# A recurrence with a feed-forward network on one core: another issue order for the first third of the pieces

## The chip, the cores and the metric

The kernel runs on one core of a Trainium2 chip. The metric is the device time of one execution in microseconds (us); lower is better. The engines are named as in the profile: PE is TensorE's matmul, PEld its weight load, DVE is VectorE, ACT ScalarE, POOL GpSimd and SP SyncE, which only issues DMAs here. Each engine works off its own queue strictly in order; an instruction at the head that waits for another engine holds everything behind it.

## What is computed

Two blocks follow each other. The first is a recurrence over 768 steps on a 40 × 40 state for each of 4 × 8 heads:

```python
for t in range(S):
    kt, vt, rt = (k[:, :, t], v[:, :, t], r[:, :, t])
    wt, at, bt = (w[:, :, t], a[:, :, t], b[:, :, t])
    y[:, :, t] = np.einsum('bhd,bhde->bhe', rt, state)
    Sa = np.einsum('bhde,bhe->bhd', state, at)
    state_decay = state * wt[:, :, None, :] - np.einsum('bhd,bhe->bhde', Sa, bt)
    state = state_decay + np.einsum('bhd,bhe->bhde', vt, kt)
```

The second takes the 3072 tokens of 8 × 40 = 320 values through an RMS norm and a SwiGLU network of 1536 hidden units:

```python
rms = np.sqrt(np.mean(x * x, axis=-1, keepdims=True) + 1e-06)
xn = x / rms * rms_g
g = xn @ w_gate
silu = g * (1.0 / (1.0 + np.exp(-g)))
val = xn @ w_val
return (silu * val @ w_out).astype(np.float32)
```

The inputs of the recurrence are float32; the three weight matrices arrive as 64-bit floats and are narrowed to float32 on the chip.

## The kernel before

**Stages.** The 768 steps are cut into 24 chunks of 32. For each chunk c there are three stages. `front(c)` (L652) loads w, a, k and b, transposes them on TensorE, builds products over spans of 2, 4, 8 and 16 steps (K, A and Ab tiles, T for the decays), makes Gram matrices in PSUM ("gramk") and picks their masked parts into LT (`where`, the COPY_PREDICATED of the profile). It then stores LT to DRAM (tile sB) and loads it back in another layout as M. `inverse(c)` (L760), or for the first four chunks `early_inverse(c)` (L778), solves the triangular system of a chunk: a chain of short multiply and subtract pairs on VectorE, then a store to sY, a load back, and for the early chunks two groups of small matmuls ("inv"). `main(c)` (L810) applies the state, solves for the chunk's updates, updates the state and computes the output tokens, which it normalizes and transposes into xg. After every second chunk `feed(g)` (L939) takes 256 tokens through the network: for each of the 12 slices of hidden units it loads a slice of narrowed weights from sW and runs the matmuls "h64", "h" and "out".

**Narrowing.** `narrow(f, h)` (L973) makes one half of such a weight slice: two to four loads of raw 64-bit words on SP into a wf tile, three activations on ScalarE (the first reads the top 16 bits, `ex<-wf,ctop`), one tensor_scalar and two scalar_tensor_tensor on VectorE, and a store to sW. It runs once for each half slice and is spread over the first part of the program.

**Constants.** At the start GpSimd makes two index rows with `iota` (L537), from which VectorE makes the masks msk and near; GpSimd also fills the pads and fixed parts of tiles (`blank`, L478, the MEMSET rows of L479; `pcopy`, L475, the COPY rows of L476).

**Order.** None of these functions issues anything by itself. Each operation, or each group of matmuls with one purpose, becomes a piece in a `Plan` (L244), which notes what the piece reads and writes (`add`, L280). After all stages have been entered, `issue` (L322) emits the pieces in the order of the string `ORDER` (L33). A number n stands for the n-th piece after the first one that is not yet out, so 0 is the next in the order of entry; "-" issues one warm-up matmul (L1015), which multiplies the identity into a spare part of a PSUM tile. `PAIRS` (L228) has a digit for each use of PSUM: which of the three pairs of banks (ps0 to ps2) it gets. As each engine takes its instructions in program order, the string fixes the order of every engine's queue, and the order of DMAs on SP, ACT and POOL. The DMAs of the first chunks are issued from SP and ACT, later ones from POOL.

The diff touches the two strings alone; they are consumed here:

```python
        for word in order.split():
            if word == "-":
                self.order.append(None)
                self.warm()
                continue
            i = first + int(word)
```

Of the kernel before, what the change touches and what calls it, by code (L numbers as in the profile page):

```python
# [33 lines left out]
85 83 84 76 58 78 86 74 73 59 60 75 5 89 61 88 77 4 43 6 201 7 87 334 90 44 8 214 213 53 62 9 - - - - - - - - 93 18 10  # L34
567 335 557 11 12 13 79 14 15 94 566 80 210 16 95 558 108 17 200 - - - 97 96 19 20 100 21 2 22 101 23 98 25 568 202 24
26 107 112 57 - - - - - 102 106 111 124 27 209 122 392 103 109 52 119 113 104 54 578 569 577 155 199 125 110 105 204
120 - - - - - - 114 203 118 117 121 559 211 598 589 562 46 131 129 132 45 560 212 597 563 588 561 123 115 136 586 384
133 134 - - - - - 126 130 116 47 564 3 145 216 394 383 135 336 128 137 48 144 143 141 91 587 219 142 51 570 127 1005
565 146 138 337 55 573 579 281 393 220 582 608 571 390 234 239 607 572 583 580 380 574 251 222 38 221 609 575 581 42 -
- - - - - - - 223 82 226 339 64 379 227 338 39 81 139 224 263 149 576 238 153 56 249 247 590 206 584 228 382 237 591  # L40
593 272 40 233 232 381 154 0 593 32 139 390 204 228 591 388 234 249 247 - - 324 235 35 31 27 244 229 146 147 259 281
245 258 149 34 325 594 36 33 270 155 243 62 605 584 598 230 - 239 40 214 599 601 242 628 64 49 91 627 602 30 626 1135
600 28 48 257 603 29 241 68 150 255 65 0 1347 194 0 194 84 173 0 - - - 182 540 200 0 184 1 186 542 540 0 506 0 457 469
849 199 455 242 111 97 110 112 96 51 61 439 460 458 122 50 243 0 0 255 242 0 709 104 470 242 120 246 259 708 57 247
458 456 0 257 718 256 470 242 0 716 265 487 486 0 268 0 0 265 101 473 0 262 277 0 273 0 236 0 260 0 269 0 242 461 - -
- - - - - 237 0 240 0 278 242 252 0 242 252 0 90 0 0 98 99 246 0 0 230 440 0 230 94 93 457 440 231 - - - - - - - - -
240 441 244 0 44 0 468 440 255 0 450 468 269 469 0 257 214 439 238 213 203 0 257 203 93 449 92 0 0 234 - - - - - - - -
245 437 0 250 262 0 464 246 247 436 260 245 446 258 259 469 244 - - 255 471 465 468 470 466 0 269 215 255 478 466 93
94 264 95 96 266 97 0 97 470 1 2 98 99 0 0 96 467 97 469 98 468 251 265 99 470 100 471 101 441 102 103 258 104 105 260
106 - - - - - - - - - - - 0 106 107 471 108 0 108 502 503 472 0 108 109 110 111 0 0 0 0 0 - - 13 0 16 562 572 146 571  # L50
561 147 14 142 143 374 15 13 355 - - - 25 386 358 0 358 386 388 16 25 387 389 390 70 79 17 391 28 191 147 355 356 80
148 149 359 0 68 28 2 29 149 0 149 34 150 29 151 187 24 25 31 152 33 153 188 391 393 32 154 35 390 392 358 0 0 152 40
187 153 27 154 155 156 33 157 158 159 160 161 34 162 36 163 164 37 165 41 391 38 42 392 39 394 561 166 395 393 552 0
42 559 549 548 395 209 0 549 560 42 165 210 43 44 211 427 428 395 - - - 565 166 45 167 557 168 0 565 566 168 739 0 522
693 534 526 124 - - 0 526 124 139 0 535 681 682 579 0 535 545 547 140 536 138 141 0 547 545 555 543 578 0 558 520 567
- - - - - - 518 378 0 696 378 380 381 695 518 120 685 526 - - - - - - 522 686 379 527 382 136 530 383 554 529 121 - -
141 540 523 565 539 537 142 538 524 - - - - 145 525 148 534 149 152 154 551 535 147 555 - - 157 146 550 536 150 155
# [3 lines left out]
478 595 568 - - 35 830 594 567 820 38 36 - 476 37 571 366 570 0 605 356 433 434 435 436 120 437 0 317 318 319 320 441  # L61
321 322 323 355 456 324 458 459 442 4 357 325 457 326 327 443 328 0 443 328 329 330 331 357 0 35 0 330 2 37 450 359 3
36 358 331 332 357 333 356 0 462 330 461 464 448 331 332 468 364 447 463 31 467 476 458 333 365 334 335 0 425 439 441
302 426 436 0 6 439 2 0 435 332 2 436 443 444 0 448 332 442 334 443 333 340 449 0 32 297 329 342 330 - 3 338 33 341
334 0 332 331 0 332 293 441 0 438 0 436 293 333 336 295 337 309 438 338 1 375 342 310 365 374 515 27 292 0 362 26 28
44 339 29 34 292 27 32 338 0 646 29 34 336 32 0 439 64 315 647 646 339 440 441 63 340 0 287 413 312 313 623 12 414 314
415 315 416 608 624 32 417 480 418 625 419 420 421 316 626 638 33 0 312 417 625 418 - - - - 476 313 601 602 600 610
812 419 420 421 822 258 422 423 0 313 810 423 625 637 2 0 819 2 0 254 473 420 421 645 310 422 0 - - - - - 310 422 3
313 33 0 28 626 307 419 639 627 420 637 308 0 637 20 635 420 647 21 421 23 422 613 648 819 38 22 809 423 39 659 24 611
3 612 36 818 424 651 808 621 425 25 660 426 - 616 249 427 0 427 3 25 58 57 428 28 47 0 428 429 28 430 3 431 0 26 25  # L70
614 484 31 27 617 627 0 458 216 400 590 600 401 0 12 582 32 401 583 25 0 397 579 21 - - - - - - - - - 588 29 28 30 591
22 453 428 398 605 23 0 591 23 429 602 24 609 0 24 397 588 602 1 604 398 429 430 2 399 427 0 584 - - - - - - - - - - -
- - - 4 397 0 25 397 4 0 393 394 21 23 27 28 395 598 24 424 607 0 21 38 35 395 37 396 24 2 424 47 397 398 399 400 25
# [4 lines left out]
663 729 634 977 562 563 717 713 986 978 665 564 565 566 975 567 568 714 569 985 570 571 967 722 572 723 - 0 400 403  # L78
726 402 572 401 573 0 726 738 736 573 739 574 664 575 737 576 577 3 723 578 751 579 760 580 747 581 582 633 583 584 0
584 585 3 634 586 636 587 635 734 588 633 0 746 588 - - - - - 403 757 589 722 590 3 404 591 592 593 594 595 596 408  # L80
# [967 lines left out]
```

## Time and profile before

| | |
|---|---|
| three runs | 1069.33, 1063.34, 1067.66 us |
| median of the three | 1067.66 us |
| the profiled execution, its own time | 1062.36 us |
| its span in the profile | 1060.6 us |
| mean granted TensorE clock in it | 0.979 |
| PE idle over the span | 51.1 us (1060.6 − 1009.5) |

The profile describes one execution. Times in it count from the start of its span. "Idle before" an instruction is the time its engine stood still ahead of it, with the instruction that ended the wait. In the row of forty slices each digit is a tenth of a slice of 26.5 us. DVE and DMA look like this over the forty slices:

```profile
DVE  8978878776868988898898798989889899787411
DMA  9965458766565483655565555574555555443252
```

A view of stretches gives the busy time of each engine in a window of time; a view of the timeline lists instructions with their start, duration, line, tiles (out<-in) and the wait ahead of them.

### The profile page before, as it was taken

How to read it: one execution, taken by the hardware profiler on the slowest of the kernel's cores; microseconds unless marked ns; L12 is line 12 of the kernel's file. 1: busy time of each engine (PE TensorE's matmuls, PEld its weight loads, DVE VectorE, ACT ScalarE, POOL GpSimd, SP SyncE). 2: the span in 40 equal slices, each digit the busy share in tenths (PEclk: the TensorE clock that was granted, in tenths of full speed). 3: DMA queues.
4: the chain of work that ended last, by engine and by line, in shares of the span. 5: the costliest groups of instructions: out<-in, count | busy, mean ns of one | idle time of the engine just before them, and what ended most of it. 6: DMA issues, size and time to landing. Idle time of an engine off the chain costs nothing.

```text
span 1060.6 us, 53494 instructions
## 1 busy us (share of the span) xinstructions
PE 1009.5 (95%) x23406; PEld 829.3 (78%) x23406; DVE 842.3 (79%) x2861; ACT 468.1 (44%) x1043; POOL 309.5 (29%) x554
## 2 busy tenths in 40 slices
PE   7868999999999999999999999999999999999997
PEld 6767777777888778787778778787777888787875
DVE  8978878776868988898898798989889899787411
ACT  6856666643543534434443444434344443431211
POOL 8824413120532241241233241340331331110000
PEclk9777998999999999999999999999999999999999
DMA  9965458766565483655565555574555555443252
GB/s 168 216 155 133 77 127 207 211 123 178 127 140 126 106 173 96 150 134 125 123 155 129 135 132 114 122 160 119 137 126 126 138 137 138 100 132 102 80 162 68
DMA packets 172457, 143.35 MB, mean 135 GB/s; under 512 B 125504, under 2 KB 143872, under 8 KB 172224
## 3 DMA queue, kind: packets, MB, share of 16 engines
q1 hardware_dynamic: 153856, 116.96, 42.9%
q0 software_dynamic: 16192, 22.64, 12.1%
q8 instruction: 184, 3.01, 1.2%
q10 hardware_dynamic: 2176, 0.33, 0.3%
q14 instruction: 49, 0.40, 0.1%
HBM read 123.86 MB, written 15.99 MB: 132 GB/s over the span
## 4 chain that ended last, share of the span: by engine, by line
PE 72%; DVE 8%; DMA 4%; ACT 3%; issue 3%; POOL 2%; SPq 1%; DVEq 0%; ACTq 0%; POOLq 0%
PE ps L486 50%; PE po L486 13%; PE ps L489 8%; DMA wf<-sW 2%; DVE LT L444 1%; DVE y L444 1%; DVE tmp L444 1%; POOL kbn L483 1%; DVE Yi L444 1%; DVE K L444 1%; SPq L483 1%; DMA sY<-Yi 1%; ACT VU L467 1%; PE po L1015 0%; DVE Ab L444 0%
## 5 line engine op out<-in xcount | busy, mean ns | idle before, releaser
L486 PE MATMUL ps<-xg,wf 128*128 128x256 f32 (+1 forms) x1728 | 353.5, 390 | 4.0 <-DVE xg L444 2.0
L486 PEld LDWEIGHTS ps<-xg,wf 128*128 128x128 f32 (+1 forms) x1728 | 261.4, 188 | 57.2 <-issue 15.0
L486 PE MATMUL po<-wf,hT 128*128 128x320 f32 x576 | 183.1, 449 | 0.1
L464 ACT ACTIVATE sg<-ps 128x256 f32<-128x256 f32 x144 | 53.6, 382 | 228.2 <-PE ps L486 224.9
L444 DVE TENSOR_TENSOR tmp<-Yi,M 128x60 f32<-128x60 f32 (+24 forms) x620 | 130.7, 211 | 19.1 <-DMA M<-sB 5.9
L444 DVE TENSOR_TENSOR Yi<-Yi,tmp 128x60 f32<-128x60 f32 (+24 forms) x620 | 129.7, 209 | 12.7
L483 POOL DMA_DIRECT2D VU<-in_v_dram x92 | 53.2, 584 | 274.1 <-PE ps L486 141.8
L486 PEld LDWEIGHTS po<-wf,hT 128*128 128x128 f32 x576 | 102.5, 191 | 35.7 <-issue 4.1
L444 DVE TENSOR_TENSOR hT<-ps,sg 128x256 f32<-128x256 f32 x144 | 59.7, 420 | 67.2 <-ACT sg L464 66.4
L444 DVE TENSOR_TENSOR K<-K,T 128x512 f32<-128x512 f32 (+1 forms) x192 | 93.4, 496 | 8.3 <-PE ps L486 5.8
L486 PEld LDWEIGHTS ps<-Ab,K 40*64 40x64 f32 x4608 | 77.2, 138 | 28.1 <-issue 10.5
L467 ACT COPY K<-K 128x256 f32<-128x256 f32 (+1 forms) x168 | 71.7, 443 | 58.4 <-PE ps L486 39.2
L486 PE MATMUL ps<-Ab,K 40*64 40x56 f32 x4608 | 87.2, 224 | 9.7 <-issue 3.8
L444 DVE TENSOR_TENSOR As<-ps,msi 128x256 f32<-128x256 f32 (+1 forms) x186 | 78.9, 476 | 14.4 <-PE ps L486 13.8
L467 ACT COPY KN<-ps 128x640 f32<-128x640 f32 x96 | 66.1, 690 | 53.5 <-PE ps L489 23.3
L483 POOL DMA_DIRECT2D kbn<-in_b_dram x92 | 53.3, 583 | 96.7 <-PE ps L486 94.3
L486 PEld LDWEIGHTS ps<-As,KN 128*40 128x40 f32 x3072 | 66.5, 124 | 15.7 <-issue 10.4
L483 POOL DMA_DIRECT2D kbn<-in_k_dram x92 | 53.6, 585 | 82.7 <-PE ps L486 82.6
L486 PE MATMUL ps<-As,KN 128*40 128x32 f32 x3072 | 73.2, 205 | 3.1 <-issue 2.5
L483 POOL DMA_DIRECT2D wn<-in_w_dram x92 | 51.6, 567 | 62.7 <-DVE tmp L444 24.1
L444 DVE TENSOR_TENSOR y<-y,ps 128x256 f32<-128x256 f32 x119 | 50.0, 420 | 16.2 <-PE ps L486 13.7
L444 DVE COPY_PREDICATED LT<-near,ps 128x384 f32<-128x384 uint32 (+2 forms) x72 | 52.2, 725 | 2.6 <-PE ps L486 2.0
(133 smaller groups left out, 1546.0 us busy)
## 6 DMA issues: line engine op xcount, KB each, us to landing
wf<-sW SPq DMA_DIRECT2D x144, 480.0 KB, 3.9
M<-sB SPq DMA_DIRECT2D x80, 128.0 KB, 4.1
rn<-in_r_dram SPq DMA_DIRECT2D x24, 160.0 KB, 5.4
sW<-ex SPq DMA_DIRECT2D x16, 240.0 KB, 3.4
out_dram<-o SPq DMA_DIRECT2D x48, 80.0 KB, 4.2
kbn<-in_k_dram POOLq DMA_DIRECT2D x92, 40.0 KB, 3.9
kbn<-in_b_dram POOLq DMA_DIRECT2D x92, 40.0 KB, 4.1
wan<-in_a_dram POOLq DMA_DIRECT2D x46, 80.0 KB, 4.9
```

The costliest lines, as they stand in the source:

```text
L444: plan.add("DVE", kind, lambda at: fn(at(o), *m(at)), [o], aps(*args))
L464: plan.add("ACT", "act", lambda at: nc.scalar.activation(at(o), at(a), f, **kw), [o] + aps(acc), [a])
L467: plan.add("ACT", "copy", lambda at: nc.scalar.copy(at(o), at(a)), [o], [a])
L483: plan.add(by, "dma", lambda at: queue.dma_start(out=o, in_=i), [o], [i])
L486: return o, lhsT, rhs, lambda at: nc.tensor.matmul(at(o), lhsT, rhs, start=start, stop=stop, skip_group_check=True)
L489: return o, i, ident, lambda at: nc.tensor.transpose(at(o), i, ident)
```

## The change

`ORDER` and `PAIRS` are replaced; 198 lines go and 198 come, and nothing else differs. The code that enters the pieces is the same, so every piece does the same work on the same tiles.

```diff
 ORDER = """
-85 83 84 76 58 78 86 74 73 59 60 75 5 89 61 88 77 4 43 6 201 7 87 334 90 44 8 214 213 53 62 9 - - - - - - - - 93 18 10
-567 335 557 11 12 13 79 14 15 94 566 80 210 16 95 558 108 17 200 - - - 97 96 19 20 100 21 2 22 101 23 98 25 568 202 24
...
+85 84 83 53 57 43 60 5 4 78 86 76 74 73 89 75 88 6 213 201 44 51 58 7 77 87 334 - - - - - - - - 93 8 9 10 11 12 13 567
+80 - - - 97 589 578 79 557 558 335 577 569 568 566 95 94 96 98 107 18 14 15 16 17 19 20 21 22 23 25 100 101 26 108 111
...
 PAIRS = """
-0120112210001221012012210211000102102120201021100221210111012202202000111100112120100012102221212201000112001120122221
...
+0120112020001221012022120211000102120110002021100201020111010201102101011122222020100012211121221211000121011220111012
...
 """
```

Of 6179 words the first 2347 are another order of the same set: 2196 pieces and 151 warm-ups. The last 3832 words issue the same pieces in the same order as before; their PSUM pairs 0 and 2 are exchanged. Counted by engine, among the reordered pieces are 266 of PE, 951 of DVE, 441 of ACT, 252 of POOL and 286 of SP. PE keeps 196 of its 266 in place and moves none by more than four places. The other queues move by 3.3 (DVE), 2.4 (ACT), 5.6 (POOL) and 2.0 places (SP) on average, and by up to 53, 38, 47 and 22. The two iotas on POOL now stand ahead of one of the Ab copies. The memsets of wn, ST and LT that stood at POOL's places 35 to 37 stand at 20, 9 and 28. The first activation of the first narrowed half slice stands at ACT's place 13 in place of 17, and the four sB stores of chunk 0 at SP's places 32, 33, 41 and 42 in place of 34, 37, 38 and 39. Places count each engine's own queue from the first reordered word.

More of the change, by code (lines that the diff above doesn't have):

```diff
@@ L39 @@
[L39 to L53, printed above, removed]
@@ L62 @@
[L62 to L71, printed above, removed]
@@ new lines @@
+80 - - - 97 589 578 79 557 558 335 577 569 568 566 95 94 96 98 107 18 14 15 16 17 19 20 21 22 23 25 100 101 26 108 111
+112 24 - - - - - 102 106 113 214 46 47 27 209 210 59 212 200 48 383 62 199 61 38 52 586 82 588 587 3 598 2 109 103 123
+104 110 105 121 559 560 119 120 122 124 134 - - - - - - 114 117 118 125 133 562 116 136 145 561 570 131 115 137 129
+130 146 563 135 - - - - - 126 132 143 128 211 55 202 203 204 71 336 219 141 127 564 597 565 1005 90 608 91 606 138 579
+571 220 221 222 580 338 142 581 337 572 339 582 583 573 226 227 234 239 574 238 139 144 590 251 584 249 593 575 247
@@ new lines @@
+237 216 155 45 281 41 33 392 384 36 393 206 380 54 69 282 390 28 - - - - - - - - 223 153 224 228 154 591 233 140 248
+250 592 260 147 148 585 576 627 607 81 609 0 149 148 262 593 231 228 234 235 258 243 242 594 229 271 - - 324 41 71 378
+38 390 388 64 39 270 1135 325 598 599 244 600 245 230 - 239 601 602 91 261 609 381 29 69 204 30 63 380 393 67 36 155
+214 151 150 625 603 260 254 240 612 269 255 98 613 - - - 251 610 241 611 256 257 1413 595 604 627 628 1005 616 617 0
+370 238 239 225 240 250 371 372 373 251 128 586 129 130 131 224 132 385 133 377 390 134 135 235 37 5 179 21 849 850
@@ new lines @@
+188 178 20 34 840 189 6 839 3 0 11 0 191 483 484 238 242 266 0 99 0 0 249 250 0 260 0 0 0 232 256 258 458 241 271 0
+254 266 0 - - - - - - - 234 238 0 0 239 0 239 97 99 98 96 439 460 461 232 0 0 0 244 230 243 231 - - - - - - - - - 240
+260 451 271 439 246 440 452 441 86 245 0 44 0 451 0 258 0 438 0 0 448 0 436 234 265 200 211 201 210 91 90 - - - - - -
+- - 245 437 251 463 0 463 254 249 247 447 248 465 259 246 464 260 261 234 0 469 470 471 468 436 261 244 465 94 466 0 -
+- 254 269 215 255 478 466 94 264 266 95 270 96 97 0 97 470 2 1 98 99 0 0 96 467 97 98 468 469 99 470 100 471 101 441
@@ new lines @@
+260 102 103 104 105 106 - - - - - - - - - - - 0 106 107 471 108 0 108 502 503 472 256 0 108 109 110 111 248 0 0 0 0 0
+- - 13 0 571 561 572 562 146 147 142 143 374 16 15 14 13 386 - - - 25 355 387 0 388 357 358 389 16 25 387 390 80 70 69
+17 391 28 147 355 356 148 191 36 359 149 0 78 2 0 187 24 27 25 148 149 32 30 150 151 152 153 154 29 358 391 390 392
+188 155 156 33 157 158 159 160 393 2 0 187 25 34 33 158 32 159 28 160 161 162 36 163 37 164 165 38 41 40 391 394 166
+395 392 39 0 392 209 166 41 395 42 558 549 548 561 551 550 0 42 43 44 45 211 166 167 395 427 428 - - - 565 558 559 0
@@ new lines @@
+566 565 167 168 571 0 522 124 - - 0 526 124 139 0 162 535 546 548 0 535 531 536 522 681 690 0 679 0 139 138 - - - - -
+- 518 378 379 687 696 689 576 577 697 686 519 380 0 135 136 380 541 543 545 557 553 381 526 382 - - - - - - 522 527
+523 530 538 524 525 529 120 383 121 - - 141 142 - - - - 145 534 537 154 149 152 148 540 536 147 146 535 550 - - 157
+155 153 151 150 165 0 159 690 678 160 161 162 163 2 555 538 551 1 553 550 0 443 510 433 44 427 45 46 47 48 424 511 513
+512 3 1 2 0 554 564 555 563 566 556 45 421 432 437 436 422 435 438 433 571 996 995 434 442 572 0 45 0 571 439 441 442
@@ new lines @@
+584 576 438 827 572 45 445 577 46 587 837 828 838 573 446 47 48 11 12 575 444 443 0 48 597 599 573 - - 49 582 0 38 36
+37 0 - 475 477 566 573 572 583 585 570 569 433 434 435 581 436 365 366 829 355 819 820 830 356 120 0 441 355 316 317
[3 rows of a table added]
+338 - 3 33 0 0 328 431 337 293 336 0 440 439 438 437 296 294 337 328 338 329 339 330 0 330 309 1 0 363 362 373 372 290
+44 35 34 33 32 338 337 339 25 26 0 26 307 512 339 27 440 28 441 0 441 28 339 442 315 0 618 616 608 617 287 414 311 415
+416 417 312 418 419 313 623 420 421 314 315 480 624 625 626 316 5 6 35 261 12 34 0 25 415 416 417 418 419 631 420 421
@@ new lines @@
+310 623 422 26 - - - - 474 599 598 311 600 608 0 311 312 475 809 819 808 818 422 623 423 0 633 423 632 424 634 425 642
+0 253 - - - - - 311 4 312 313 644 642 26 314 425 0 425 33 0 28 0 639 637 421 647 422 651 423 23 24 21 0 21 612 423 610
+2 611 620 3 647 247 38 24 817 808 818 807 424 425 659 25 58 57 37 35 426 427 428 - 615 0 618 428 3 429 27 622 430 621
+431 30 488 0 0 219 7 17 18 404 3 405 587 406 588 407 601 603 0 603 0 625 458 216 26 27 404 0 404 584 597 28 - - - - -
+- - - - 593 34 0 28 30 27 22 0 0 426 398 22 399 601 1 451 2 23 602 588 604 430 603 427 608 428 429 24 0 - - - - - - -
@@ L234 @@
+1110000100022112102200121100022000022011001112110101001010020111001200020022111122211120000212222022012211111112011010
+2111221121012020220101000011221201011100220122222011221212222110122222110000102020110100221222010122002212201220000101
+1010112210022022222101102000200011111011110211102122222200121211002101122111200021002211122110022222120222200010212000
+012202021212122122210120120
 """
```

21 lines of the change are left out of this document (4 added, 17 removed), and 304 rows, old and new, of the table ORDER.

## The prediction

> **What bounds the kernel now.** First the head of the page (span, busy shares, the clock's row), then the chain that ended last, then the busy time of five stretches of the first third.
>
> ```profile
> span 1060.6 us, 53494 instructions
> PE 1009.5 (95%) x23406; PEld 829.3 (78%) x23406; DVE 842.3 (79%) x2861; ACT 468.1 (44%) x1043; POOL 309.5 (29%) x554
> PEclk9777998999999999999999999999999999999999
> ...
> PE 72%; DVE 8%; DMA 4%; ACT 3%; issue 3%; POOL 2%; SPq 1%; DVEq 0%; ACTq 0%; POOLq 0%
> ```
>
> TensorE is busy 95% of the span; only the first slices of its clock row show 7s and 8s. The stretches (length, then busy time of PE, PEld, DVE, ACT, POOL; granted clock; DMA share; GB/s):
>
> ```profile
> 0.00:25.00 25.00, 18.32 (x345) 16.98 (x345) 20.41 (x55) 14.76 (x28) 21.68 (x48) 1.00 0.94 170
> 25.00:50.00 25.00, 20.57 (x399) 17.93 (x399) 23.68 (x68) 22.48 (x48) 23.30 (x51) 0.73 0.88 207
> 50.00:75.00 25.00, 18.18 (x487) 16.58 (x488) 22.75 (x80) 13.90 (x28) 3.81 (x7) 0.84 0.81 187
> 75.00:100.00 25.00, 21.20 (x696) 19.00 (x699) 17.40 (x59) 13.60 (x28) 10.29 (x20) 0.68 0.53 129
> 100.00:350.00 250.00, 240.83 (x5788) 197.46 (x5787) 195.42 (x645) 131.33 (x297) 74.77 (x130) 0.99 0.60 144
> ...
> 176.20:183.10 6.90, 6.77 (x86) 4.62 (x86) 6.90 (x19) 3.60 (x8) 0.00 (x0) 0.51 0.60 189
> ```
>
> Until 75 us VectorE (82, 95, 91% busy) sets the pace; GpSimd is as full to 50 us and the DMA engines are 81 to 94% busy. TensorE is idle 21.7 us before 100 us (100 − 18.32 − 20.57 − 18.18 − 21.20), and its busy time there holds the 151 warm-up matmuls. From 100 to 350 us it is idle 9.2 us (250 − 240.83), clock 0.99: there it is the bound. Replaying both orders against the pieces, the last 3832 words issue the same pieces, with PSUM pairs 0 and 2 exchanged, from some 330 to 370 us on. So the change can win at most those 31 us of idle time and what half clock costs: five stretches, 44.4 us in all, 37.5 of them before 98 us, where VectorE sets the pace, and 6.9 in the last row, where TensorE does.
>
> **The change part by part.** No instruction is added or removed: 2196 pieces and 151 warm-ups stand in another order. TensorE's own order hardly moves (196 of its 266 pieces keep their place, none goes further than four, the warm-ups stay between the same pieces), so each gain must come through an input that is ready sooner.
>
> *1. Start of VectorE.* Its first mask operation starts at 4.80 us, when GpSimd's second iota is done (4.62 + 0.15). Now both iotas stand ahead of an Ab copy of 0.71 us: −0.7. But one of the first A products now stands behind more mask operations; I take −0.4 for the start as a whole (−0.7 to +0.2).
>
> *2. The blocked tensor_scalar.*
>
> ```profile
> 22.54 3.38 DVE L444 TENSOR_SCALAR wf<-wf 128x480 int32<-128x480 int32 x2
> 22.92 0.65 POOL L479 MEMSET wn<- 128x640 f32 x1
> 23.49 0.97 POOL L479 MEMSET ST<- 128x1024 f32 x1
> ```
>
> Of these two, the first took 2.92 us, while memsets of wn, ST, LT and M (0.65, 0.97, 0.54, 0.33) ran on GpSimd; two others of the form before 30 us took 0.43 and 0.55, later ones 0.41. The wn, ST and LT memsets move from GpSimd's places 35, 36, 37 to 20, 9, 28, so up to 2.5 us (2.92 − 0.41) can go. But a new run without DMA issues stands at places 34 to 38: memsets of M, kbn and M, an eye select and a msi copy, 0.33 + 0.44 + 0.33 + 0.44 + 0.45 = 2.0 us. By its place it falls at 21 to 23 us, where VectorE now has two such tensor_scalars in places 50 and 52. In the bad case 2.0 − 0.4 = 1.6 us of the gain is lost again. I take −1.5 (−2.5 to +0.5, the latter if both are blocked).
> [...]
>
> *3. The weight conversion on ScalarE.* This is the edit that costs.
>
> ```profile
> 14.29 0.41 ACT L467 COPY K<-K 128x256 f32<-128x256 f32 x1 [0.47 <-DVE K L444]
> 15.40 0.40 ACT L467 COPY K<-K 128x256 f32<-128x256 f32 x1 [0.71 <-DVE K L444]
> 16.81 0.74 ACT L464 ACTIVATE ex<-wf,ctop 128x480 f32<-128x480 int16 x1 [1.00 <-DMA wf<-in_moe_w_out_dram]
> ...
> wf<-in_moe_w_gate_dram SPq DMA_DIRECT2D x3, 256.0 KB, 5.0
> wf<-in_moe_w_out_dram SPq DMA_DIRECT2D x3, 224.0 KB, 6.7
> ```
>
> The first conversion act moves from ScalarE's place 17 to 13, ahead of two Ab and two K copies. It needs SP's loads of 256 and 224 KB; before, the second came in at 16.8. In SP's new order a 224 and a 64 KB load go ahead of them, and 160, 96 and 40 KB (an rn half, a w_out, a VU) fall behind: 8 KB less in front. At the 170 GB/s of this stretch that is 0.05 us, but the order of issue shifts too; I take a landing at 16.3 (15.3 to 18.3: one issue slot or one such load's time, 256 KB at 170 GB/s = 1.5 us, and some on top). ScalarE's last copy ends at 12.24, so it is parked 4 us, where its idle pieces came to 3.3 before. Behind the parked act stand its second step (0.69), K copies (0.4 each) and Ab copies (0.3 each): the last Ab copy ends at 16.3 + 0.74 + 0.69 + 0.81 + 0.59 ≈ 19.1. VectorE reaches the product that reads it, now in place 38, at 16.5 to 17: a stall of 2.2 us in order. Before, VectorE lost 0.78 us near there to the same load: the conversion's tensor_scalar, now in place 39, no longer waits. So +1.4 (0 to +4).
>
> *Sum at the end of front(0):* −0.4 − 1.5 + 1.4 = −0.5. Its last LT mask (29.47 to 29.90, place 61, now 59) ends at about 29.4 (27.4 to 32).
>
> *4. The round trip of LT on SP.*
>
> ```profile
> 29.93 0.33 SPq L483 DMA_DIRECT2D sB<-LT  x1
> 32.03 2.76 SPq L483 DMA_DIRECT2D sB<-LT  x3
> ...
> 40.24 0.43 SPq L483 DMA_DIRECT2D M<-sB  x1
> ```
>
> The four sB stores go from SP's places 34, 37, 38, 39 to 42, 32, 33, 41. Two of them now queue behind two narrow stores that wait for VectorE's last conversion steps (before, 0.64 us steps ending at 28.6 and 31.4), and four loads and a column of gcol: the last store goes out at about 35.5 instead of 33.1 to 34.8. But the two M loads now follow almost directly (places 44 and 45, one wn load between), where 1.46 us of a weight load stood before them. M was in SBUF at 44.7; I take 44.4 (43.2 to 45.7). Two VU halves and a wn piece change places as well; VU is needed at 34 by main(0)'s first matmul and now issued at 25, and landed in 4.5 us: hidden, by about 4 us, and if that cover is gone it delays main(0) as many us as it is late.
>
> *5. inverse(0) and main(0).*
>
> ```profile
> 66.62 0.20 POOL L479 MEMSET M<- 128x128 f32 x1 [7.08 <-DMA sY<-M]
> 67.17 1.85 SPq L483 DMA_DIRECT2D M<-sY  x4
> 70.95 0.79 PE L486 MATMUL ps<-M,LT 16*16 16x16 f32 x64 [4.21 <-DVE tmp L444]
> ```
>
> VectorE's other work between the first and the last step of inverse(0) adds up to 17.9 us before and 18.15 after: +0.2. The steps behind it (store, memset, four loads, matmul) keep their order. The 4.21 us is TensorE idle, the largest such wait: it moves one for one with inverse(0), −0.3 + 0.2 − 0.4 (narrow work that moved behind the chain) = −0.5 (−2 to +2.5).
>
> *6. From 75 to 350 us.* VectorE's work ahead of most TensorE steps is 0.4 to 2 us less, but TensorE has 9.2 us of idle time there, in pieces under 2 us, and its own work covers the rest. I take −0.6 (−2 to +0.5); the moves of ScalarE, GpSimd and SP there are taken at nothing, under the cover of TensorE's queue; if the cover goes, a TensorE step waits as long as its input is late, and 1.0 to 2.0 us is what such waits cost before.
>
> The first four parts end in the M of part 4 and are not added again. Sum: −0.5 − 0.6 = −1.1. The profiled execution took 1062.36, so 1061.3 by its side. That execution lies 5.3 below the median of the three runs (1067.66); all four average 1065.7, and I set the forecast against this: **1064.6 us**.
>
> **The rivals.**
> *B, the block on VectorE goes in full and nothing is handed back.* For it: the four memsets that stood beside the 2.92 us are gone from there. Against: part 3's stall. It gives −2.5 − 0.4 − 0.6, and with the head earlier the 6.9 us of half clock at 176 us (worth 3.4) may not come: 1065.7 − 6.9 = 1058.8.
> *C, slower: ScalarE waits at the first conversion act.* Its loads come 2 us later than I take, because DMA is 94% busy and SP's issues are reshuffled; the stall on VectorE is 4.2, not 2.2, the tensor_scalar is blocked as before, the sB stores go out 1.2 later, and M and inverse(0) come 3.2 us later. TensorE waits longer than 4.21 ahead of inverse(0)'s matmul, and another 10.2 us at half clock (the length of two of the five stretches) falls into TensorE-bound time, at 5.1. It decides from a landing after about 17.5 us. 1065.7 + 3.2 + 5.1 = 1074.0. For it: the order has ScalarE, not VectorE, waiting; against: 8 KB less stands in front of the loads.
> *D, nothing shows.* TensorE's order is the same and its slack takes up all: 1065.7.
> [...]
>
> **How the numbers follow.** Forecast 0.42, B 0.25, C 0.26, D 0.07. About 0.5% (5.3 us) is what a measurement of this kernel can tell from no change: under 1062.3 is faster, over 1073.0 slower. Faster: most of B (0.22) and a quarter of the forecast's own spread (0.10), 0.32. Slower: three quarters of C and a little of the forecast (0.20 + 0.02), 0.22. Within: 0.46. The range reaches below B and just past C, 1057.5 to 1074.5; the forecast's own is 1060.5 to 1069.
>
> **What would show it.** Right: the first mask operation at 4.1 us; the longest tensor_scalar under 2.5; ScalarE idle some 4 us ahead of its first conversion act, released by a load, and a wait of about 2 on VectorE for an Ab copy; M's step at 44 to 45; inverse(0)'s matmul at 70 to 71; TensorE's idle time from 100 to 350 us near 9. Wrong: that matmul over 2 us off, or a shift of the whole that arises after 100 us with TensorE idle there in new places.

## The result

Ten executions of each, taken in turn: the changed kernel has a median of 1072.38 us (1068.67 to 1075.97), the kernel before 1064.93 (1062.27 to 1069.33). The ratio is 1.0072, with a 95% interval of 1.0051 to 1.0093: slower by 0.7%, which is little but clear of its interval, where 1064.6 and a small gain had been forecast. Measured again against the kernel before on three later occasions, on three chips, the changed kernel came to 1.0014 (0.9979 to 1.0050), 1.0037 (0.9999 to 1.0076) and 1.0059 (1.0024 to 1.0093). The ratios leave out executions over 1.5% above the fastest of their kernel and are not quotients of the medians given beside them (the two can differ by 0.3%). So the order costs something between nothing and 0.7%. Whether the four differ by the chip, by the occasion or by chance was not separated; what goes with a longer execution of the same kernel is shown below.

The head of the page of the changed kernel; its profiled execution took 1072.73 us:

```profile
span 1070.9 us, 53483 instructions
PE 1013.9 (95%) x23406; PEld 833.4 (78%) x23406; DVE 840.1 (78%) x2861; ACT 466.4 (44%) x1043; POOL 309.3 (29%) x554
PEclk9687989999999999989999999999999999999999
q8 instruction: 184, 3.01, 1.2%
PE 72%; DVE 7%; DMA 4%; issue 4%; ACT 2%; POOL 2%; SPq 1%; DVEq 0%; ACTq 0%; POOLq 0%
```

TensorE is busy 4.4 us longer (1013.9 against 1009.5) with the same 23406 matmuls, and idle 5.9 us longer. The chain now has 4% under "issue", 3% before. The same stretches as before the change (length; busy time of PE, PEld, DVE, ACT, POOL; clock; DMA share; GB/s):

```profile
0.00:25.00 25.00, 15.82 (x278) 14.53 (x278) 20.53 (x51) 12.04 (x24) 24.04 (x54) 1.00 1.02 167
25.00:50.00 25.00, 21.54 (x450) 19.14 (x451) 23.51 (x66) 21.75 (x45) 18.13 (x39) 0.67 0.80 173
50.00:75.00 25.00, 18.64 (x472) 17.31 (x471) 23.25 (x84) 15.96 (x33) 7.40 (x16) 0.91 0.80 200
75.00:100.00 25.00, 19.27 (x676) 17.14 (x676) 17.51 (x60) 13.20 (x25) 8.90 (x17) 0.73 0.57 138
100.00:350.00 250.00, 239.40 (x5770) 197.92 (x5771) 188.79 (x635) 129.71 (x297) 73.34 (x127) 0.97 0.58 141
```

The late start is plain in the first row: 278 matmuls by 25 us against 345. By 50 us most of it is made good (728 against 744), but inverse(0)'s first matmul starts at 72.15 instead of 70.95. From 100 to 350 us the mean clock is 0.97 instead of 0.99. The stretches at half clock behind 100 us, taken one by one:

```profile
102.00:105.40 3.40, 3.40 (x46) 3.30 (x34) 2.06 (x6) 3.00 (x10) 2.17 (x4) 0.50 0.46 70
132.70:139.50 6.80, 6.80 (x169) 5.50 (x160) 3.55 (x16) 1.28 (x5) 0.76 (x2) 0.50 0.13 21
156.60:160.00 3.40, 3.40 (x12) 2.29 (x11) 2.08 (x6) 0.29 (x1) 0.00 (x0) 0.50 0.97 253
337.50:340.90 3.40, 3.40 (x42) 2.47 (x40) 3.40 (x12) 0.00 (x0) 0.87 (x2) 0.50 0.53 159
460.40:467.20 6.80, 6.80 (x85) 5.04 (x78) 4.29 (x16) 0.69 (x1) 0.00 (x0) 0.50 0.14 24
```

23.8 us in all, against 6.9 before, with TensorE busy in every one of them. At half of that time they would cost some 8.5 us ((23.8 − 6.9) / 2) more than before, by estimate; as TensorE's busy time grew by 4.4 us only, not all of it is left in the 10.3 us between the two spans. The last stretch lies where the change moved nothing.

Where the 10.3 us arise is seen when the two profiles are matched by the count of TensorE's matmuls. The same matmul comes 1.6 us later than before at 100 us (times of the kernel before), 1.5 at 319, 6.8 at 339, 6.0 at 447, 11.1 at 491, and the last one 10.5. So what the three stretches between 100 and 160 us cost is made good by 319 us, and the loss comes at two places, around 336 and 460 us, at the last two stretches of the list.

Ahead of each stretch TensorE had stood still, and it is these rows that matter most. The timeline of TensorE at four of the places; in brackets the idle time and what ended it:

```profile
98.11 0.38 PE L486 MATMUL ps<-M 16*32 16x16 f32 x24
99.97 0.53 PE L486 MATMUL ps<-M 16*32 16x16 f32 x40 [1.49 <-issue]
...
129.56 0.34 PE L489 MATMUL ps<-ident,ST 104*104 104x104 f32 x2
131.35 0.70 PE L489 MATMUL ps<-ident,ST 104*104 104x104 f32 x6 [1.46 <-issue]
...
333.14 0.71 PE L486 MATMUL ps<-VU,KN 64*40 64x40 f32 x53
336.00 0.31 PE L486 MATMUL ps<-VU,KN 64*40 64x40 f32 x10 [2.16 <-issue]
...
457.15 0.49 PE L486 MATMUL ps<-Ab,K 40*64 40x56 f32 x17
459.60 0.86 PE L486 MATMUL ps<-Ab,K 40*64 40x56 f32 x44 [1.96 <-issue]
```

The queue stops inside a group of equal matmuls on the same tiles (at the third place 53 of them had run from 333.14 us on), and the profile shows no engine or data transfer that released it. What it waited for, by the counts that follow, is its own program. Count TensorE's rows (weight loads, matmuls, waiting instructions) in order of start, from 0: behind 95 us every stop of over 0.5 us that ends on "issue" comes at a number that is 193 modulo 256, or at the row after it, in both kernels (3777, 5569, 14785 and 20417 here). The queue q8 moves 3.01 MB in 184 packets, 16 KB each, and TensorE has 47139 rows: 256 instructions a packet. In neither profile does the first instruction of a block start less than 1.18 us after its packet has landed. For block 56 (brought by packet 56, counted from 0), whose first instruction is number 14785, the packet of the changed kernel moves from 333.84 to 334.77 and the matmul starts at 336.00; before, it moved from 326.44 to 327.38, 3.9 us ahead of its need. DMA in the 3.3 us ahead of that late packet, and in the 2.2 us behind:

```profile
DMA packets 417, 1.04 MB, mean 314 GB/s; under 512 B 62, under 2 KB 190, under 8 KB 417
q1 hardware_dynamic: 417, 1.04, 85.3%
...
q8 instruction: 1, 0.02, 2.7%
```

The 16 engines were 85% filled with SP's transfers (weights for feed and two output stores), and the instruction packet went as soon as they had drained: the last of their packets ended at 333.84 us, where its own move begins.

### The profile page after: what moved, and what is told of

It is laid out like the page before. It is cut to its first block, busy times and chain, and to the rows that moved or that the text cites. A ratio compares the mean times of both kernels' runs of the same rounds, so it can differ in the third digit from the quotient of the medians.

```text
span 1070.9 us, 53483 instructions
## 1 busy us (share of the span) xinstructions
PE 1013.9 (95%) x23406; PEld 833.4 (78%) x23406; DVE 840.1 (78%) x2861; ACT 466.4 (44%) x1043; POOL 309.3 (29%) x554
## 3 DMA queue, kind: packets, MB, share of 16 engines
q8 instruction: 184, 3.01, 1.2%
## 4 chain that ended last, share of the span: by engine, by line
PE 72%; DVE 7%; DMA 4%; issue 4%; ACT 2%; POOL 2%; SPq 1%; DVEq 0%; ACTq 0%; POOLq 0%
PE ps L486 50%; PE po L486 13%; PE ps L489 8%; DMA wf<-sW 1%; POOL kbn L483 1%; DVE tmp L444 1%; SPq L483 1%; PE po L1015 1%; DVE As L444 1%; DVE Yi L444 1%; DVE y L444 1%; DVE LT L444 1%; DMA wf<-in_moe_w_out_dram 1%; DVE K L444 1%; DMA wf<-in_moe_w_gate_dram 1%
## 5 line engine op out<-in xcount | busy, mean ns | idle before, releaser
L486 PE MATMUL ps<-xg,wf 128*128 128x256 f32 (+1 forms) x1728 | 359.1, 396 | 2.9 <-DVE xg L444 1.6
L486 PEld LDWEIGHTS ps<-xg,wf 128*128 128x128 f32 (+1 forms) x1728 | 264.5, 191 | 57.8 <-issue 14.3
L486 PE MATMUL po<-wf,hT 128*128 128x320 f32 x576 | 181.5, 447 | 0.3 <-DVE hT L444 0.3
L486 PEld LDWEIGHTS po<-wf,hT 128*128 128x128 f32 x576 | 102.0, 190 | 35.9 <-issue 3.9
L486 PEld LDWEIGHTS ps<-Ab,K 40*64 40x64 f32 x4608 | 77.6, 138 | 32.6 <-issue 13.1
L486 PE MATMUL ps<-Ab,K 40*64 40x56 f32 x4608 | 87.7, 225 | 13.3 <-issue 4.6
L486 PEld LDWEIGHTS ps<-As,KN 128*40 128x40 f32 x3072 | 66.4, 125 | 17.0 <-issue 9.3
L486 PE MATMUL ps<-As,KN 128*40 128x32 f32 x3072 | 73.1, 205 | 4.6 <-issue 2.6
```

The lines of the kernel that those rows point to most:

```text
L486: return o, lhsT, rhs, lambda at: nc.tensor.matmul(at(o), lhsT, rhs, start=start, stop=stop, skip_group_check=True)
```

## The experiments

Two theories at first. **F**: the loss lies behind 75 us, in instruction loads that land late and the half clock behind them. **H**: the late head shifts everything. All ratios are to the kernel before, executed in turn with each.

**Parts of the order.** Four kernels take a part of the new order and the rest of the old one. Each engine's queue can be taken over whole:

```diff
 L467 TensorCopy K_142<-K_141 128x512
+L464 Activation ex_177<-wf_167,ctop 128x480
+L464 Activation ex_177<-ex_177,cmid 128x480
 L467 TensorCopy K_141<-K_142 128x16x4x4 x2
...
```

(ScalarE's queue in the first of them.) VectorE and ScalarE new:

> VectorE and ScalarE take the new order, TensorE, GpSimd and SP keep the old one (the two can only be exchanged together). Theory F (the loss lies behind 75 us: TensorE's instruction loads land late behind other transfers, TensorE stands still in the middle of groups of matmuls and the clock halves after it; what moved those transfers is the new order of SP and GpSimd): within 2 us of the kernel before, 1063 to 1067. Theory H (the loss is the late start: ScalarE parked at the first conversion, products late on VectorE; everything after shifts with it): most of the loss, 1069 to 1073.

1086.27 (ratio 1.0216, 1.0185 to 1.0247): outside both. The two engines' new order does not fit the old order of transfers; TensorE waits 3.55 us at 88.8 and 3.18 us at 162.6 for what comes late. This run tells nothing of the two theories, except that the queues were ordered to each other.

> GpSimd and SP, so all the memsets and nearly all the transfers, take the new order; TensorE, VectorE and ScalarE keep the old one. Theory F: the loss is here, 1069 to 1074, with TensorE standing still 1 us or more in the middle of matmul groups behind 95 us at least three times. Theory H: at most the part that a blocked tensor_scalar costs, 1065 to 1068. If both this and the other half lie near the kernel before, the two halves only cost together.

1066.89 (1.0023, 1.0000 to 1.0045): in H's range and below F's. Its profile has one stop of over 1 us on "issue" behind 95 us (1.22 us), where F had asked for at least three.

Then a cut in time, in place of one by engine:

```diff
 ORDER = """
-85 83 84 76 58 78 86 74 73 59 60 75 5 89 61 88 77 4 43 6 201 7 87 334 90 44 8 214 213 53 62 9 - - - - - - - - 93 18 10
+85 84 83 53 57 43 60 5 4 78 86 76 74 73 89 75 88 6 213 201 44 51 58 7 77 87 334 - - - - - - - - 93 8 9 10 11 12 13 567
...
```

> The new order up to inverse(0)'s first group of matmuls (some 72 us), from there the old one for what is left. Theory H: the whole loss, 1070 to 1074. Theory F: only the late head, 1.2 to 2 us, 1065 to 1068.

1063.80 (0.9991, 0.9963 to 1.0019). Its profile has inverse(0)'s first matmul at 72.35, as late as the changed kernel, and the whole loss, which H had for it, does not come. H falls as the main cause. The time is also under F's range, which counted the late head of 1.2 to 2 us; whether that head reaches the end is not settled, as the interval goes up to 1.0019 (2 us), and this profile is 1.6 us behind that of before at inverse(0) and 1.5 at its end.

> The old order up to inverse(0)'s first group of matmuls (some 71 us), from there the new one. Theory H: as before, 1063 to 1067. Theory F: 1068 to 1072, with the stand-stills of TensorE behind 95 us and half clock after them as in the changed kernel.

1066.45 (1.0010, 0.9979 to 1.0040). The stand-stills are there (1.96 us at 146.8, 2.70 at 329.8), as F has it, but the time is below F's range and in that of H. Neither part carries the 0.7%.

**The same kernel again**, three times in the course of the study:

> The changed kernel as it is, once more, on the chip and against the runs of before that the next kernels have too. Both theories: 1070 to 1075. Theory F (the clock is the loss): mean granted clock over its runs near 0.971, against 0.978 of before, and time times clock equal to that of before, 1042 to 1043; most stand-stills of over 1 us behind 95 us recur at the same instruction numbers of TensorE, 193 modulo 256. If they are chance alone, other places show them.

1065.32 (1.0014): below the range of both theories. Of the five stops that half clock followed in the first profile, those near 130 and 150 us recur; those near 98, 333 and 458 are absent, and so is half clock behind 160 us.

> The changed kernel as it is, a third time. The first ten executions gave 1072.6 on the mean, twelve others 1065.9, with the kernel before at 1065 and 1064. Theory F (a draw of late instruction loads and half clock, made anew with each load of the program onto a chip): anything between 1062 and 1074, and the clock goes with it, near 0.975 if under 1067 and near 0.971 if over 1070. Theory H (a steady cost of the new order): 1070 to 1074.

> The changed kernel as it is, on the same chip as the next three. Ratio to the kernel before between 1.001 and 1.007; where its profile has TensorE standing still over 2 us near 330 us (instruction 14785 of its stream) with half clock behind it, its time is over 1070 against 1065 of before; where not, about 1065.

1073.09 (1.0037) and 1071.71 (1.0059), here with the kernel before at 1070.67 and 1066.14. The first lies in the ranges of both theories, the second where it was expected. Both profiles have the stop at 14785 (2.43 us, and 1.61 where over 2 had been expected) and half clock behind it, and one at 20417; the profile from the occasion at 1065 has no stop of over 0.5 us at either number. So of the four profiles of this kernel, those with both stops took 1072.73, 1075.26 and 1074.52 us, and the one without 1062.62. The mean clock went with the time: 0.9714, 0.9752, 0.9723 and 0.9730 on the four occasions, 0.977 to 0.979 for the kernel before on the last three.

**Where the block boundaries fall.** Very small matmuls ahead of all work make TensorE's stream longer; they stand in place of 4 of the first 8 warm-ups (of all 8 for a whole block), and nothing else changes:

```diff
+            if word == ".":
+                self.nudge()
+                continue
...
+    plan.nudge = lambda: nc.tensor.matmul(po_[0:16, 0, DM:DM + 16], ident[0:16, 0:16], ident[0:16, 0:16], start=False, stop=False, skip_group_check=True)
```

> The changed kernel with 36 very small matmuls in place of 4 of the first 8 warm-ups, ahead of all work: TensorE's stream gets 128 instructions longer, half a block of 256, so that every later block boundary falls on another matmul; nothing else moves. Theory F: the stand-stills stay at 193 modulo 256 of the stream, so they fall on other pieces; the time is drawn anew, by 2 to 8 us, rather down (1063 to 1070), as the new order was unlucky. Theory H (a late start, order of work): 1071 to 1074, within 1.5 us of the changed kernel.

> The kernel before with the same 128 more instructions ahead of all work. Theory F: drawn anew too, rather up, 1065 to 1072. Theory H: 1063 to 1067, as before.

> The changed kernel with 20 very small matmuls in place of 4 warm-ups: 64 more instructions, a quarter of a block. Theory F: another draw, different from that of 128 by 2 us or more in one direction or the other, between 1062 and 1074. Theory H: 1071 to 1074.

> The kernel before with 72 very small matmuls in place of all 8 first warm-ups: 256 more instructions, one whole block, so that every block boundary falls on the same matmul as before. If the 53 us that 128 more instructions cost came from where the boundaries fall: 1061 to 1070, like the kernel before. If the small matmuls themselves or the missing warm-ups cost it: 1100 or more.

128 more instructions: 1117.32 (1.0507, 1.0455 to 1.0559) for the new order and 1117.82 (1.0497, 1.0446 to 1.0548) for the old one. 64 more: 1107.28 (1.0392, 1.0337 to 1.0446). 256 more, a whole block: 1067.94 (0.9975, 0.9938 to 1.0012). F's mechanism stands, and its size was far too low: no time with 64 or 128 more lies in the range of either theory. Behind 95 us the stops of over 0.5 us on "issue" are still at 193 modulo 256, or one or two rows after it, in all four. The page and the waits of TensorE for the kernel before with 128 more (lines of the kernel are three higher there, L489 is L486), and then the waits with 256 more:

```profile
span 1117.8 us, 53622 instructions
PE 1039.1 (93%) x23470; PEld 850.8 (76%) x23470; DVE 841.3 (75%) x2861; ACT 468.9 (42%) x1043; POOL 309.0 (28%) x554
PEclk9778899899998999998999999999979998999999
...
PE ps L489 <- issue: 38.6, 32, 3.0
PE ps L489 <- DVE tmp L447: 5.5, 4, 2.7
```

```profile
PE ps L489 <- issue: 19.5, 25, 1.8
PE ps L489 <- DVE K L447: 4.7, 3, 3.0
```

```profile
PE ps L486 <- issue: 16.9, 25, 1.8
PE ps L486 <- DVE tmp L444: 5.2, 3, 4.2
```

The last fence is the kernel before itself. "Issue" goes from 16.9 to 38.6 us and the clock's row has 7s and 8s as far as its last quarter; with a whole block "issue" is at 19.5. There are more of the small matmuls there (72 against 36) and fewer warm-ups, so these are not what costs. Both orders lose 5% as soon as the boundaries move by half a block: where they fell was part of what made the kernel fast. The traces show how. In the kernel before, 7 of the 173 blocks from block 10 on were passed in under 3 us, and the stops right behind these add up to 2.1 us; with 256 more it is 9 blocks and 3.0 us. With 64 or 128 more it is 26 or 27 blocks, and the stops behind them add up to 30.1 to 33.4 us. Behind all other blocks they stay at 10.8 to 13.9 us in these five profiles. So in these five profiles boundaries that left a run of short matmuls whole in one block let TensorE come to its end before it could go on with the next.

**Which edit makes block 56 late.** Seven of the eight profiles that have the new order of all queues behind inverse(0) show the stop at 14785, none with the old order of all queues there. Two candidates were moved alone, in both directions: the two output stores in the burst, and a group of h matmuls next to the boundary.

```diff
+L483 DMACopy out_dram<-o_176 32x2x320 x2
 L483 DMACopy wf_170<-sW_68 128x960
 L483 DMACopy wf_171<-sW_69 128x960
-L483 DMACopy out_dram<-o_176 32x2x320 x2
```

> The changed kernel with one edit on SP: the last two of feed(1)'s four output stores go out ahead of two of feed(2)'s weight loads, as they did before, not behind them, where they sit in the burst that holds up the instruction load of block 56. Theory F: no stand-still over 1 us at instruction 14785 and no half clock from 330 to 345 us; 3 to 5 us faster than the changed kernel beside it, ratio to before 0.998 to 1.002. Theory H, or if the burst is late anyway: as the changed kernel, within 1 us.

> The kernel before with the same two output stores moved behind those two weight loads, as in the changed kernel; all else as before. Theory F: the stand-still of some 2.4 us at instruction 14785 (in most executions) and half clock behind it appear; 2 to 5 us slower than before, ratio 1.002 to 1.005. Theory H: 0.999 to 1.001.

> The old order up to inverse(0)'s first matmuls, the new one behind it, with the two output stores early: the early head of the one, the rest of the other. If the late head (1.5 to 1.8 us at inverse(0)) and the stores are what the new order costs, this is the best of all: 1059 to 1064 where before is 1065, ratio 0.994 to 0.999.

1069.69 (1.0037, 1.0004 to 1.0071), 1065.38 (1.0022, 0.9993 to 1.0051) and 1068.85 (1.0050, 1.0019 to 1.0080). With the stores early the stop stayed (1.34 and 2.69 us); with the stores late in the old order it did not come. The changed kernel with the stores early is 2.0 us below the changed kernel beside it, between what the two theories had; the other's ratio is at the lower edge of F's range, but without the stop, and its interval includes 1. The stores are not what makes the stop, and the mixture is no better kernel.

```diff
+L486 Matmult ps_77<-xg_165,wf_168 128x256 x4
 L486 Matmult po<-wf_171,hT_174 128x320 x2
 L486 Matmult po<-wf_167,hT_175 128x320 x2
-L486 Matmult ps_77<-xg_165,wf_168 128x256 x4
```

> The changed kernel with one group of TensorE moved: feed(2)'s h matmuls (8 rows of the trace) ahead of the two out groups that stand before them, as in the kernel before; every other engine is untouched. Theory P (the out groups free the buffers whose reload fills all DMA engines; with h behind them, TensorE reaches the point that asks for block 56 just as that reload starts, and the instruction load waits behind it): the load of block 56 starts some 270 to 280 instructions ahead of its need, no stand-still over 0.5 us at instruction 14785, no half clock behind it; 2 to 5 us faster than the changed kernel, ratio to before 0.999 to 1.003. Rival Q (TensorE's own order is worth nothing): stand-still and time as in the changed kernel, 1.003 to 1.007.

> The kernel before with the same group moved the other way, behind the two out groups; every other engine is untouched. Theory P: a stand-still of 1.3 to 2.9 us at instruction 14785 and half clock behind it, ratio 1.002 to 1.005. Rival Q: no stand-still there, 0.998 to 1.001.

1069.32 (1.0034, 1.0004 to 1.0064) and 1064.82 (0.9986, 0.9953 to 1.0020). In the first the stop is still there, in the second still not:

```profile
331.71 0.71 PE L486 MATMUL ps<-VU,KN 64*40 64x40 f32 x53
334.86 0.42 PE L486 MATMUL ps<-VU,KN 64*40 64x40 f32 x10 [2.44 <-issue]
```

Theory P falls, and Q's times came out for both. The whole of TensorE's order exchanged:

> The changed kernel with the whole of TensorE's order as it was before (266 pieces, 52 pairs of which the change had exchanged); the four other engines keep the new order. Theory P: as new_h_first or better, 0.998 to 1.003. Rival Q: 1.003 to 1.007.

> The kernel before with TensorE's new order and the four other engines' old one. Theory P: as old_h_last or worse, 1.002 to 1.007, with the stand-still at 14785. Rival Q: 0.998 to 1.002; waits of TensorE for VectorE where the two orders do not fit may add up to 2 us in either theory.

1071.00 (1.0089, 1.0058 to 1.0121) and 1078.98 (1.0124, 1.0074 to 1.0174): both slower than P or Q had it. The second is clearly worse than the order that it was made from; the first is not clear of the 1.0072 that the changed kernel had at its first measurement. TensorE waits for data in new places (1.66 us for As, up to 340.9, in the one, 1.88, up to 347.3, in the other): as with VectorE and ScalarE, a queue out of its set costs more than the effect that was looked for. The stop at 14785 is absent in the first and there in the second (1.60 us). It does not hang on TensorE's order alone, though: the first kernel above (VectorE and ScalarE new), with TensorE's old order, has it too (1.57 us, ended at 355.74), and one profile of the changed kernel has not. Which pieces make it stays open.

What the profiles with the stop share is the time of the packet. Of the 17 profiles whose boundaries were not moved by part of a block, nine have the stop: in these packet 56 moves 1.6 to 3.5 us after TensorE has begun the block before, and data fill 61 to 86% of the DMA engines in the 4 us ahead of it. In the eight without (with 256 more it is packet 57), it moves from 3.0 us before that point to 0.3 after, with 26 to 45%. The 4 us ahead of the packet in the changed kernel, and in the profile of the same kernel without the stop:

```profile
329.84:333.84 4.00, 4.00 (x133) 3.48 (x132) 3.72 (x14) 2.20 (x5) 0.00 (x0) 1.00 0.80 276
323.52:327.52 4.00, 4.00 (x137) 3.06 (x136) 2.58 (x10) 1.64 (x6) 0.00 (x0) 1.00 0.42 125
```

Here the packet went either ahead of a burst of transfers or behind it, and in the same kernel it was the one or the other (DMA share 0.42 and 0.80 in these rows).

## Where the time went

For each kernel its profiled execution: its time; TensorE's stops of over 0.5 us at a block boundary in three stretches, in us with their number; and the time at half clock in the same stretches.

```
                 us      stops 75-300  300-500   500-     half clock 0-75  75-300  300-500
old order behind inverse(0)
before           1062.36   5.8 (5)    2.6 (4)  2.9 (3)        21.6   22.8    0.0
old_h_last       1061.12   5.8 (6)    1.8 (2)  1.9 (2)        20.7   17.0    0.0
old_stores       1062.97   6.6 (8)    1.9 (3)  4.3 (4)        21.7   12.4    0.0
old_shift256     1068.65   9.1 (7)    1.8 (2)  1.9 (2)        14.6   23.0    0.0
head_new         1064.01   8.5 (8)    1.2 (2)  1.9 (2)        34.1   23.9    0.0
new order behind inverse(0)
changed kernel   1072.73   7.8 (7)    5.8 (4)  3.7 (4)        20.8   26.9   10.2
again_new        1062.62   7.4 (6)    0.8 (1)  2.0 (3)        32.3   22.4    0.0
again_new2       1075.26  10.6 (10)   5.8 (4)  4.0 (4)        27.3   17.1   10.3
again_new3       1074.52  12.1 (9)    4.4 (3)  2.5 (3)        34.0   20.6   10.3
new_stores       1069.62   8.9 (8)    3.8 (3)  3.8 (4)        30.8   23.8    3.4
new_h_first      1069.70   9.4 (9)    4.2 (3)  1.6 (3)        20.1   14.2   10.2
head_old         1065.10   8.9 (9)    5.0 (3)  2.8 (3)        21.2   16.5    6.8
mixed_stores     1070.97   9.7 (9)    3.8 (2)  3.4 (3)        26.8   17.6    3.4
boundaries moved
new_shift64      1113.97  17.5 (11)  10.1 (5) 11.4 (12)       34.2   47.7    6.8
new_shift128     1111.36  15.2 (11)  11.5 (6) 15.3 (13)       30.6   30.8   20.5
old_shift128     1119.55  15.7 (11)   9.5 (6) 16.8 (13)       24.1   26.9   13.6
```

Means of the five against the eight: the stops from 75 to 300 us go from 7.2 to 9.4, those from 300 to 500 from 1.9 to 4.2, and half clock there from 0 to 6.8 us, which costs half of it, 3.4, by estimate. That is 7.9 us (2.2 + 2.3 + 3.4); the profiled times differ by 6.2 on the mean (1070.1 − 1063.8). So 5.7 of the 7.9 us sit between 300 and 500 us, and from 350 us on the order there is the old one word for word. Matched by the count of matmuls, the eight are on the mean 0.4 us behind the five at 319 us, 5.1 at 339, 5.6 at 447, 7.6 at 491 and 6.3 at the end. So what the stops up to 300 us cost is made good, some 4.7 us arise around block 56, and some 2 around 460 us.

What carries it there is shown in part. The stop at 14785 lies in the reordered part. For what lies behind, one more difference was found: the new order has more places in which TensorE needs a separate waiting instruction, 327 rows of its sequencer against 313. From some 350 us on, its unchanged stream is therefore 14 instructions further along, and every boundary falls on another matmul. Sorted by that distance: 0 or 1 more instructions, and a whole block, gave 0.9986, 0.9991 and 0.9975; 2 and 8 more 1.0022 and 1.0023; 12 more 1.0010 and 1.0050; 14 more 1.0014 to 1.0072 in six measurements; 78 more (64 and these 14) 1.0392; 128 and 142 more 1.0497 and 1.0507. The three kernels in which a single queue or pair of queues was exchanged out of its set and TensorE waited for data (1.0216, 1.0124, 1.0089) stand outside this row. That so few as 14 cost anything is argued from this row and not shown. Most of these intervals overlap, the same rows separate the old order from the new, and most of the loss, at block 56, goes with the burst ahead of the packet. Against it stands the kernel with TensorE's old order among new queues, which has 12 more: its profile has 0.7 us of stops and no half clock between 300 and 500 us. The kernel before with 14 more instructions and no other change wasn't tried.

## Why the prediction was wrong

*Part 1 and part 2, the mask operations and the blocked tensor_scalar.* The first mask operation starts at 3.92 (4.1 was forecast) and the conversion's tensor_scalars take at most 0.65 us: as forecast, the 2.9 us block is gone from there. It came back earlier. The second tensor_scalar of VectorE's mask operations and GpSimd's work beside it:

```profile
4.36 2.94 DVE L444 TENSOR_SCALAR vut<-vut 128x32 int32<-128x32 int32 x1
5.15 0.44 POOL L479 MEMSET kbn<- 128x384 f32 x1
5.50 0.97 POOL L479 MEMSET ST<- 128x1024 f32 x1
6.39 0.86 POOL L479 MEMSET A<- 128x896 f32 x1
```

It ends with the last of the memsets, at 7.3. Where both terms together were to bring 1.9 us, the A products start 1.5 us later, at 11.84 instead of 10.31, and what the conversion gives back comes only behind them. The forecast looked for a new run of GpSimd's beside the conversion (places 34 to 38) and not beside the mask operations, where memsets of kbn, ST and A now stand. The two rows of 2.9 us, one in each kernel (2.92 and 2.94), each last over several memsets in a row; the median of the seven tensor_scalars on vut is 0.18 us. What held VectorE there is not shown beyond that.

*Part 3, ScalarE.* Almost to the tenth: parked 4.08 us until the load landed at 16.18 (4 us and 16.3 forecast).

```profile
16.18 0.74 ACT L464 ACTIVATE ex<-wf,ctop 128x480 f32<-128x480 int16 x1 [4.08 <-DMA wf<-in_moe_w_out_dram]
...
23.98 0.69 DVE L444 TENSOR_TENSOR K<-K,T 128x512 f32<-128x512 f32 x1 [1.56 <-ACT K L467]
```

The stall of 2.2 us on the Ab copy did not come (between 12 and 23.9 us VectorE has no wait of over 0.15 us), as VectorE itself was late by then; 1.56 came at 24 us, for a K copy queued behind the next conversion's first act, which was parked 1.85 us for its own load. The last LT mask of front(0) ended at 30.45, 0.5 late where 0.5 early was forecast.

*Parts 4 and 5.* The last sB store went out at 37.1 (35.5 forecast), yet inverse(0) began on VectorE at 44.71 instead of 45.09, as M was there (44.4 was forecast for it). From there to the end of its last step it took 1.1 us longer, where VectorE's other work was to add 0.2, and ended 0.7 later; the stores, the memset and the loads behind it then took 11.8 us, 11.3 before, where 0.4 less was forecast. The matmul came 1.2 us later, not 0.5 earlier.

```profile
69.03 0.20 POOL L479 MEMSET M<- 128x128 f32 x1 [8.28 <-DMA sY<-M]
72.15 0.22 PE L486 MATMUL ps<-M,LT 16*16 16x16 f32 x6 [2.48 <-DMA M<-sY]
```

That is the mis-sized half, 1.7 us off. The profile of the changed kernel is still 1.5 us behind at 319 us; that the head makes the loss is what head_new excludes.

*Part 6, "From 75 to 350 us … −0.6".* This is the step that failed, with the premise it rests on: that with TensorE's order nearly kept each gain or loss must come through an input that is ready sooner or later. An input that no engine makes, the instruction itself, decided: stops at a block boundary from 300 to 500 us came to 5.8 us, 2.6 before. From 76 to 362 us of the kernel before, the changed kernel's profile fell back by 4.7 us (from 1.5 to 6.2), where −0.6 was forecast, and behind 362 us, where nothing was, by another 4.3. The row that said so stood in the profile of before: TensorE waited 16.9 us for "issue", the largest of its waits, and the forecast put no price on it. "No instruction is added or removed" did not hold either: the pieces are the same, but TensorE's stream has 14 more waiting instructions. And where the forecast ended, at the last moved word, the loss went on; that this is because a stream 14 instructions longer meets its boundaries elsewhere is argued, not shown. The forecast's own sign of being wrong came: a shift that arises after 100 us, with TensorE idle in new places (10.6 us from 100 to 350 us, 9.2 before).

*The rivals.* C's time, 1074.0, was nearest, and that is luck, as it was not by its mechanism: the loads landed at 16.2, well ahead of the 17.5 from which it was to decide. Its second half, more half clock in time that TensorE sets, is what happened (10.2 us from 300 to 500 us, none before), by another cause. B's block did go and was handed back. Terms as large as the 3.4 of B and the 5.1 of C also come and go with the same kernel: the four profiles of the changed one took 1062.62 to 1075.26, with 0 to 10.3 us of half clock from 300 to 500 us.

## What to carry to other kernels

When TensorE's idle time is put down to "issue" and falls inside groups of equal matmuls, count its rows: stops that share one remainder modulo 256 (193 here, with 256 rows to a packet of 16 KB) point at the program's own loading. Two things brought it out here: blocks of short matmuls that were passed in under 3 us, and a burst of transfers ahead of the packet. The order that was found by measuring held for some positions of the boundaries only: 64 and 128 more instructions ahead of it cost 3.9 and some 5%, as the stops stayed at 193 or up to two rows after it and so fell on other matmuls. Any edit that adds or takes away instructions on that queue, a waiting one among them, moves the boundaries so, and an edit should be compared with a few lengths of padding, and in several measurements apart from one another. Price a moved memset against every VectorE operation that it comes to lie beside, not only against the one it is moved away from: here the row of 2.92 us went and one of 2.94 came.

## What had not been expected of the hardware

Half a block of 128 instructions, 36 tiny matmuls in place of four warm-ups, cost some 53 us, and a whole block nothing that could be measured (0.9975, 0.9938 to 1.0012). Stops of 1.1 to 2.2 us were at times followed by half clock: each of the five stretches behind 100 us began 0.8 to 2 us after the end of such a stop and lasted 3.4 or 6.8 us. They were not always: the kernel before has one of 1.84 us that ends at 208.0, the changed kernel one of 1.24 at 715.6, and no half clock follows either. What sets the lengths, and which stop is followed by half clock, is not shown.
